# Adaptive layer norm, local attention and MLP on one core: half k-tiles of the first MLP product in 64-row tiles, singly given PSUM banks, norms on two engines

## The chip, the cores and the metric

One core of one Trainium2 chip runs the whole kernel. Five engines work side by side, each through its own list of instructions in order: TensorE (PE, matrix products into PSUM; the profile shows its weight loads as PEld), VectorE (DVE), ScalarE (ACT), GpSimd (POOL) and SyncE (SP, which issues most DMAs). The metric is the device time of one execution in microseconds, the median of several runs.

## The reference, cut to what matters

```python
mod = (silu(c) @ w_mod).reshape(1, 6, 1, 448)          # c is one row of 448
sa, ca, ga, sb, cb, gb = (mod[:, i] for i in range(6))
h = layernorm(x) * (1 + ca) + sa                       # x is 2048 x 448
q, k, v = split(h @ wqkv)                              # 16 heads of 28
logits[s, w] = q[s] . k[s - 2 w] * 28 ** -0.5          # w = 0..7; masked where s - 2 w < 0
x = x + ga * (softmax(logits) applied to v) @ wo
h = layernorm(x) * (1 + cb) + sb
x = x + gb * (gelu(layernorm(h) @ w1 + b1) @ w2 + b2)  # w1 is 448 x 1792, w2 1792 x 448
```

All inputs and the output are bfloat16.

## The kernel before, in words

**Tiles.** The 2048 tokens are put in an order in which even ones come before odd ones, so that the stride of 2 in the attention becomes 1. They are 16 blocks (`b`) of 128 tokens. The 448 features are `KT` = 4 k-tiles of 128 rows, the last of which holds 64. The weights and all activations between stages stay in SBUF.

**Stages.** In the opening c, the first x and the first weights are loaded; `ps_c` and `c_col` turn c into a column, `silu` follows, and `ps_sa`, `ps_ca` (`col_fn`, L453) make sa and ca as columns, which `mod1` (L459 to L462) copies out. `front_end` takes x in groups of 2, 2, 4, 4, 4 blocks: statistics (L396, L406), `rstd` (L413 on DVE, L416 on POOL), `normalize` (L421) into `zbuf`, a transpose by PE (L517) or by DMA, modulation into `hT` (L526 on ACT, L529 on DVE), and the eight products `qk` (L539) that are copied to qT and kT (`copy`, L384 on DVE, L386 on ACT). `mod_item` (L563) makes the four other modulation vectors; ga and gb are multiplied into wo and w2. `attention(g)`, 17 times over 121 queries: logits `lt` (L613), exp (L624), mask product (L633), `pv` (L648), `po` (L658), division (`on`, L669), transpose `pt` (L679), copy `ot`. `wo_item` (L700) and the residual (L705) follow for each block, and `norm_items` for each two: two layer norms, with a modulation between them, and a DMA transpose (L739) into `yT`.

**The MLP** (`mlp_items`) is done in four chunks of 512 tokens. `w1_c.q`, for seven q, makes two of the 14 output tiles of 128 rows: four k-tiles each, so eight matmuls of 512 columns (L755). In the last k-tile, rows 0 to 63 are features 384 to 447, row 64 (`KA`) is b1 with a constant one in `ybuf`, and the rest is zero. One GELU (L762) takes both tiles, 1024 columns. `w2_b.q` (L778) adds them up for each of four blocks, and `fin`, `out` finish a block.

**PSUM** is eight banks. Pool `ps_lt` has two tiles of two banks (logits, x transposes, w1 outputs), `ps_s` three of one bank (all else), `ps_p2` one (w2's sums).

**The order** is made at build time. Each step is an operation in `Plan`, with the engines that can do it and a cost for each, what it needs, and the buffers that it takes. `order` is a list scheduler: it picks the operation that can start first, less a small weight for what lies behind it, with the hand-given offsets `PRI` and `NUDGE`; an operation with two engines gets the one that would end first by these costs. `LANDS` are assumed times at which loads have landed. `PHASES` tells how many attention steps come ahead of each chunk's w1. The engines run the resulting lists in order, and on the chip an operation waits for what it needs.

Of the kernel before, what the change touches and what calls it, by code (L numbers as in the profile page):

```python
# [16 lines left out]
KT = 4  # L17
KA = 64
# [14 lines left out]
PHASES = [9, 14, 17, 17]  # L33
W2S = [(0, 5), (5, 10), (10, 14)]
SLOTS = {"lt": 2, "s": 3, "p2": 1, "et": 2, "on": 2, "vb": 3, "z2": 2, "yT": 2, "hm": 2}

LANDS = [("c", 3.0), ("x0", 5.0), ("x2", 5.8), ("wmsa", 6.4), ("wmca", 7.2), ("wk", 8.4), ("wq", 9.4), ("later", 10.0),
         ("wv", 10.4), ("x4", 12.5), ("wmod2", 18.0), ("wo", 19.5), ("b2", 20.5), ("x8", 22.0), ("w1", 28.0),
         ("w2", 33.0)]

NIDLE = [11, 4]
PLANS = None

LOOK = 0.000121

PRI = {"ad": -181.5, "agfst": -82.1, "ags2": -347.3, "ex": -137.9, "ge": -154.4, "h": -94.5, "lt": 209.3,
       "mk": -29.7, "ml": 177.8, "on": -459.2, "po": -127.9, "pv": -157.8, "r2": 73.3, "r3": -46.8, "s2": -114.2,
       "s3": -56.5, "ve": 41.4, "w1": -75.6, "w2": -12.0, "wo": 472.9, "wq": 377.0, "x1": 437.8, "y": -137.1,
       "yt": 24.4, "z": -134.6, "z2": 11.3, "zt": 143.7}

NUDGE = {"ad12": 15.6, "ad2": -30.3, "ad8": 44.8, "agfst12": -48.8, "agfst6": 98.9, "ags2_13": -79.7,
       "ags2_14": 66.3, "ags2_15": -24.2, "ags2_2": 13.3, "ags2_8": 84.1, "ags3_13": 100.2, "ags3_14": -12.2,
       "ex14.1": 144.5, "fin2": 21.9, "ge2.0": -4.6, "ge3.3": -73.9, "h2.2": 280.0, "lt10": 82.1, "lt8": -96.4,
       "mk16": -4.1, "mk3": 236.6, "ml0": 45.3, "ml12": 24.2, "ml6": -123.2, "on16": -89.1, "on4": -65.7,
       "on9": 60.2, "ot11": 20.9, "ot2": 66.5, "ot3": -126.0, "ot4": -23.7, "out1": 36.4, "out14": 29.2,
       "out15": -322.5, "out2": 24.7, "out9": -87.4, "po16": 38.4, "po9": 49.4, "pt16": 16.3, "pt2": 36.7,
       "pt3": -118.5, "pv13": -326.1, "pv16": 12.1, "qe0.0": 77.8, "qe0.6": -60.5, "qe12.5": 124.2,
       "qe2.5": 111.3, "qe8.0": 142.3, "qe8.3": 117.4, "qk2.5": 255.7, "qk8.0": 142.4, "qk8.1": 138.6,
       "r2_10": 7.9, "r2_12": 207.3, "r2_14": 18.8, "r2_14a": 2.8, "r2_4a": 155.1, "r2_8": -68.9, "r2_8a": 87.6,
       "r3_0a": -13.7, "r3_10a": -65.1, "r3_12": -63.0, "r3_12a": 43.9, "r3_14": 28.5, "r3_14a": -10.2,  # L60
       "r3_8": -10.6, "rd15": 41.6, "rd16": -89.1, "s2_1": 61.5, "s2_12": -57.7, "s2_13": -42.9, "s2_15": -4.9,
       "s2_3": 68.8, "s2_9": -35.4, "s3_12": 65.1, "s3_14": 46.0, "w1_0.6": 31.3, "w1_1.5": 58.9,
       "w1_3.3": -59.1, "w2_0.6": 121.6, "w2_1.4": 61.0, "w2_11.0": 60.4, "w2_11.3": -105.2, "w2_11.4": -4.4,
       "w2_11.5": 45.1, "w2_11.6": 30.7, "w2_12.5": -140.6, "w2_13.2": -158.9, "w2_14.1": -6.6, "w2_14.3": -1.2,
       "w2_14.4": 47.8, "w2_14.5": 147.1, "w2_2.5": 20.1, "w2_4.2": -47.2, "w2_5.2": -7.0, "w2_5.3": -24.7,
       "w2_5.5": 19.2, "w2_5.6": -17.6, "w2_6.1": 3.9, "w2_6.2": 12.3, "w2_6.6": 5.9, "w2_8.0": -68.8,
       "w2_8.3": -69.5, "w2_8.5": 91.6, "w2_9.3": 69.1, "wo1": 88.2, "wo12": -28.3, "wo2": 44.1, "x1_1": 34.4,
       "x1_13": -39.6, "x1_3": -114.7, "y1": 51.8, "y10": 10.9, "y12": 102.0, "y13": -21.9, "y14": 13.4,
       "y3": 128.0, "yt12": -52.1, "yt13": 30.6, "yt14": 12.1, "yt9": 260.3, "z2_1": 79.9, "z2_12": 15.9,
       "z2_13": 66.8, "z2_14": 106.9, "z2_15": 45.5, "z2_4": 123.4, "z2_6": -29.2}  # L70
# [9 lines left out]
class Plan:  # L80
# [8 lines left out]
    def add(self, name, eng, needs=(), after=(), uses=(), allocs=(), lag=0.09, tab=None, at=0.0, fn=None, pri=0.0):  # L89

        i = len(self.ops)
        self.index[name] = i
        self.ops.append(dict(name=name, eng=eng, needs=list(needs), after=list(after), allocs=list(allocs), lag=lag,
                             tab=tab, at=at, fn=fn, pri=pri + PRI.get(re.match(r"[a-z]+([0-9](?=_))?", name)[0], 0.0) +
                             NUDGE.get(name, 0.0)))
        for b in list(uses) + list(allocs):
            self.bufs[b][1].append(i)

    def order(self, hop=0.07, table=1.3, win=3.413):
# [27 lines left out]
        tab = None  # L127
# [6 lines left out]

        def slot_time(t, extra=0):
            k = len(turn[t]) + extra - self.slots[t]
            if k < 0:
                return 0.0
            b = turn[t][k] if k < len(turn[t]) else None
            if b is None or any(end[u] is None for u in users[b]):  # L140
                return None
            return max(end[u] for u in users[b]) + hop

        while ready:
            best = None
            for i in ready:
# [7 lines left out]
                ok, cntt = True, {}  # L154
                for b in o["allocs"]:
                    tg = tag_of[b]
                    st = slot_time(tg, cntt.get(tg, 0))
                    cntt[tg] = cntt.get(tg, 0) + 1
                    if st is None:
                        ok = False  # L160
                        break
                    t = max(t, st)
# [4 lines left out]
                s = max(t, free[e])  # L167
# [3 lines left out]
                if best is None or key < best[0]:  # L171
                    best = (key, i, e, s)
            assert best is not None, [ops[i]["name"] for i in ready]
            _, i, e, s = best
            o = ops[i]
            d = o["eng"][e]
            if e == "PE":
                w = int(s / win)
# [11 lines left out]
            for b in o["allocs"]:  # L190
                turn[tag_of[b]].append(b)
# [14 lines left out]
def kernel(  # L206
# [39 lines left out]

    cst = ctx.enter_context(tc.tile_pool(name="cst", bufs=1))
    ps_lt = ctx.enter_context(tc.tile_pool(name="ps_lt", bufs=2, space=bass.MemoryType.PSUM))
    ps_s = ctx.enter_context(tc.tile_pool(name="ps_s", bufs=SLOTS["s"], space=bass.MemoryType.PSUM))
    ps_p2 = ctx.enter_context(tc.tile_pool(name="ps_p2", bufs=SLOTS["p2"], space=bass.MemoryType.PSUM))  # L250

    def ps_att(shape, dtype, name):
        return ps_s.tile(shape, dtype, name=name, tag="s")

    ps_small = ps_att
# [35 lines left out]
    b2_bc = cst.tile([128, D], BF16, name="b2_bc")  # L291
    silu_bf = cst.tile([128, KT], BF16, name="silu_bf")
# [9 lines left out]
    wmod = stp.tile([128, KT, 2, D], BF16, name="wmod")  # L302
    wqk_st = stp.tile([128, KT, 2 * D], BF16, name="wqk_st")
    nc.scalar.dma_start(out=x_all[:, 0:2, :], in_=xv[:, 0, 0:2, :])
    load_ktiles(nc.sync, wmod[:, :, 0, :], w_mod[:, 0:D], 0)
    load_ktiles(nc.scalar, wmod[:, :, 1, :], w_mod[:, D:2 * D], 0)
    nc.scalar.dma_start(out=x_all[:, 2:4, :], in_=xv[:, 0, 2:4, :])
    load_ktiles(nc.sync, wqk_st[:, :, D:2 * D], A_wqkv[:, D:2 * D], 0)
    load_ktiles(nc.sync, wqk_st[:, :, 0:D], A_wqkv[:, 0:D], 0)
# [4 lines left out]
    nc.sync.dma_start(out=b2_bc[:], in_=B_b2.partition_broadcast(128))  # L314
    nc.sync.dma_start(out=x_all[:, 8:NBLK, :], in_=xv[:, 1, :, :])
# [6 lines left out]
    def idle(n):  # L322
        for i in range(n):
            idle_ps = ps_att([128, 512], FP32, "idle_ps")
            nc.tensor.matmul(idle_ps[:], lhsT=idle_in[:, 0:128], rhs=idle_in[:], start=True, stop=True)

    idle(4)
# [5 lines left out]
    nc.vector.memset(w1_s[64:128, KT - 1, :], 0.0)  # L333
    nc.gpsimd.memset(neg_half[:], -0.5)
    warm = stp.tile([128, 1], FP32, name="warm")
    nc.scalar.activation(out=warm[:], in_=neg_half[:, 0:1], func=ACT.Exp)
    nc.gpsimd.memset(ident[:], 0.0)
# [28 lines left out]
    nc.vector.memset(ca1_col[64:128, KT - 1:KT], 0.0)  # L366
    nc.vector.memset(sa_col[64:128, KT - 1:KT], 0.0)
    for vb in vbufs:
        nc.gpsimd.memset(vb[:, :, DH:DH + 1], 1.0)
    for yb in ybufs:  # L370
        nc.gpsimd.memset(yb[:, D:DP], 0.0)
        nc.gpsimd.memset(yb[:, D:D + 1], 1.0)
    load_ktiles(nc.sync, w1_s, B_w1, 0)
    nc.sync.dma_start(out=w1_s[KA:KA + 1, KT - 1, :], in_=B_b1.rearrange("(o n) -> o n", o=1))
# [35 lines left out]
    def rstd(nm, tile_key, n, **kw):  # L410
        def a_fn(e):
            tv = T["tv", tile_key] = sm.tile([128, n], FP32, name="tv", tag=f"tv{n}")
            nc.vector.tensor_scalar_add(out=tv[:], in0=T["mv", tile_key][:, :, 1], scalar1=EPS)  # L413
        def fn(e):
            rs = T["rs", tile_key] = sm.tile([128, n], FP32, name="rs", tag=f"rs{n}")
            nc.gpsimd.tensor_tensor(out=rs[:], in0=T["tv", tile_key][:], in1=neg_half[:, 0:n], op=ALU.pow)  # L416
        P.add(nm + "a", {"DVE": 0.08}, fn=a_fn, **kw)
        P.add(nm, {"POOL": 0.75}, lag=0.02, needs=[nm + "a"], fn=fn)

    def normalize(dst, src, tile_key, i):  # L420
# [10 lines left out]
    def c_fn(e):  # L431
        T["ps_c"] = ps_s.tile([128, KT], FP32, name="ps_c", tag="s")
# [14 lines left out]
    def col_fn(v):  # L447
        if v == 0:
            T["ps_col"] = ps_s.tile([128, 2 * KT], FP32, name="ps_col", tag="s")
        for j in range(KT):  # L450
            nj = kr_of(j)
            for kt in range(KT):
                nc.tensor.matmul(T["ps_col"][0:nj, v * KT + j:v * KT + j + 1],  # L453
                                 lhsT=wmod[0:kr_of(kt), kt, v, j * 128:j * 128 + nj],
# [405 lines left out]
```

## Time and profile before

| | us |
|---|---|
| median of 3 runs | 190.64 (190.16 to 190.86) |
| profiled execution | 190.52 |
| its span, first to last instruction | 188.8 |
| PE busy | 179.8 (1446 matmul records) |
| DVE busy | 140.3 |
| ACT busy | 105.4 |
| first `pq` (L539) starts | 13.28 |
| first w1 product (L755) starts | 71.39 |

A group such as `L755 PE MATMUL p<-yT,w_s 128*128 128x512 bf16 x8` is eight matmuls of line 755 that use 128 rows and 128 columns of the array and move 512 columns. The busy time of a matmul is longer than the distance to the next one's start, since matmuls overlap in the pipeline; the distances tell what a matmul costs. A few matmul records are missing, so a group may count one too few. In a row of the stages (`13.00:71.00 ...`) the columns are length, then busy us and instructions of PE, PEld, DVE, ACT and POOL, then the granted clock, DMA share and GB/s.

### The profile page before, as it was taken

Reading aid. Unit: us, or ns where it says so; the run is one execution under the profiler, and the core shown is the slowest. Engines: PE = TensorE matmul, PEld = TensorE weight load, DVE = VectorE, ACT = ScalarE, POOL = GpSimd, SP = SyncE. Lnnn points to the kernel's source line nnn. Section 1 sums busy time; section 2 is a strip of 40 time slices with the busy share of each in tenths; the row PEclk is TensorE's granted clock in tenths of the full one; section 3 lists DMA queues with packets and bytes.
Section 4 is the critical chain, followed back from the end, with each engine's and each line's share of the span. In section 5 each row is a group of like instructions: output and inputs, shape, how many; then the busy total and the mean of one; then the engine's idle time right before and its main releaser. Section 6 shows DMA issues by size and latency. Waiting matters only on the chain.

```text
span 188.8 us, 3664 instructions
## 1 busy us (share of the span) xinstructions
PE 179.8 (95%) x1446; PEld 94.5 (50%) x1460; DVE 140.3 (74%) x344; ACT 105.4 (56%) x149; POOL 23.7 (13%) x53
## 2 busy tenths in 40 slices
PE   7989899899999898999999999999999999999993
PEld 2658644445544444445556544456554444444551
DVE  5688799996998999967989998399999602202451
ACT  3048687587777866558744575868364444251100
POOL 7132002200104100311030103100103100000000
PEclk9969999999999999999999999999999999999999
DMA  5999992541001150004013002120000220000021
GB/s 178 302 375 295 406 309 89 111 83 33 0 3 28 28 61 0 0 0 59 24 43 65 0 28 53 32 50 3 26 30 28 54 56 24 3 24 0 28 70 49
DMA packets 23285, 14.40 MB, mean 76 GB/s; under 512 B 13666, under 2 KB 22371, under 8 KB 23268
## 3 DMA queue, kind: packets, MB, share of 16 engines
q1 hardware_dynamic: 22244, 13.31, 26.6%
q10 hardware_dynamic: 1024, 0.86, 1.4%
q8 instruction: 11, 0.18, 0.4%
q14 instruction: 6, 0.05, 0.1%
HBM read 9.18 MB, written 1.84 MB: 58 GB/s over the span
## 4 chain that ended last, share of the span: by engine, by line
PE 72%; DVE 15%; DMA 5%; POOL 2%; issue 2%; ACT 1%; ACTq 1%; DVEq 0%
PE p L755 25%; PE p L778 23%; PE pw L700 6%; DVE st L396 5%; PE pv L648 4%; PE pq L539 4%; DMA x_all<-in_A_x_dram 3%; PE lt L613 2%; PE pt L679 2%; POOL rs L416 2%; PE po L658 2%; DMA yT<-ybuf 2%; PE ptr L517 1%; DVE hT L529 1%; DVE zbuf L421 1%
## 5 line engine op out<-in xcount | busy, mean ns | idle before, releaser
L755 PE MATMUL p<-yT,w_s 128*128 128x512 bf16 x216 | 50.5, 379 | 1.1 <-DMA yT<-ybuf 0.7
L778 PE MATMUL p<-w_s,hm 128*128 128x448 bf16 x224 | 48.3, 352 | 0.1
L762 ACT ACTIVATE hm<-p 128x1024 bf16<-128x1024 f32 x28 | 28.6, 1024 | 31.6 <-PE p L755 29.5
L624 ACT ACTIVATE et<-lt 128x1024 bf16<-128x1024 f32 x34 | 33.9, 1029 | 9.1 <-PE lt L613 9.1
L416 POOL TENSOR_TENSOR rs<-tv,neg_half 128x2 f32<-128x2 f32 (+1 forms) x21 | 20.0, 954 | 125.1 <-DVE tv L413 102.5
L755 PEld LDWEIGHTS <-w_s 128*128 128x128 bf16 x224 | 21.6, 98 | 25.9 <-issue 1.1
L778 PEld LDWEIGHTS <-hm 128*128 128x128 bf16 x224 | 21.1, 98 | 19.0
L539 PE MATMUL pq<-hT,Wqk 128*128 128x512 bf16 (+1 forms) x155 | 29.2, 335 | 0.8 <-DVE qT L384 0.6
L791 DVE TENSOR_TENSOR xt<-p,gbb_bc 128x448 f32<-128x448 f32 x11 | 6.8, 622 | 27.0 <-PE p L778 26.9
L539 PEld LDWEIGHTS <-Wqk 128*128 128x128 bf16 x160 | 15.3, 98 | 12.0 <-issue 1.1
L633 DVE TENSOR_TENSOR et<-et,mask_rest 128x2048 bf16<-128x2048 bf16 x17 | 20.6, 1209 | 0.2 <-ACT et L624 0.2
L396 DVE BATCH_NORM_STATS2 st<-x_all 128x6 f32<-128x448 bf16 x30 | 17.8, 615 | 1.6 <-DMA x_all<-in_A_x_dram 1.4
L700 PE MATMUL pw<-wo_s,oT 128*128 128x448 bf16 x64 | 14.8, 353 | 0.5 <-ACT oT L386 0.3
L648 PE MATMUL pv<-Wv,hT 128*128 128x448 bf16 x68 | 15.0, 353 | 0.0
L386 ACT CAST kT<-pq 128x512 bf16<-128x512 f32 (+1 forms) x19 | 9.6, 508 | 4.6 <-PE pq L539 4.1
L705 DVE TENSOR_TENSOR x_all<-pw,x_all 128x448 bf16<-128x448 f32 x16 | 9.8, 615 | 2.5 <-PE pw L700 2.3
L669 DVE TENSOR_TENSOR on<-po,rden 128x448 bf16<-128x448 f32 x17 | 10.5, 619 | 0.1
L386 ACT CAST vbuf<-pv 128x448 bf16<-128x448 f32 x15 | 7.8, 538 | 4.7 <-PE pv L648 4.7
L658 PEld LDWEIGHTS <-et 128*128 128x128 bf16 x272 | 9.0, 96 | 2.6 <-DVE x_all L705 0.2
L386 ACT CAST qT<-pq 128x512 bf16<-128x512 f32 (+1 forms) x18 | 9.1, 526 | 1.7 <-PE pq L539 1.2
L658 PE MATMUL po<-vbuf,et 128*128 128x29 bf16 x272 | 9.3, 176 | 0.0
L396 DVE BATCH_NORM_STATS2 st<-z 128x6 f32<-128x448 bf16 x16 | 9.2, 615 | 0.1
(101 smaller groups left out, 165.5 us busy)
## 6 DMA issues: line engine op xcount, KB each, us to landing
out_dram<-x_all SPq DMA_DIRECT2D x16, 112.0 KB, 1.7
w_s<-in_B_w_dram SPq DMA_DIRECT2D x1, 1568.0 KB, 13.4
wmod<-in_w_mod_dram SPq DMA_DIRECT2D x1, 1344.0 KB
w_s<-in_B_w_dram SPq DMA_DIRECT2D x1, 1344.0 KB, 14.4
x_all<-in_A_x_dram SPq DMA_DIRECT2D x1, 896.0 KB, 10.8
wqk_st<-in_A_wqkv_dram SPq DMA_DIRECT2D x2, 336.0 KB
x_all<-in_A_x_dram ACTq DMA_DIRECT2D x2, 224.0 KB, 4.3
x_all<-in_A_x_dram SPq DMA_DIRECT2D x1, 448.0 KB, 5.2
```

The source lines that it names most:

```text
L386: nc.scalar.copy(out=out, in_=in_)
L396: nc.vector.bn_stats(out=st[:], in_=src())
L416: nc.gpsimd.tensor_tensor(out=rs[:], in0=T["tv", tile_key][:], in1=neg_half[:, 0:n], op=ALU.pow)
L539: nc.tensor.matmul(pq[:, 0:w], lhsT=Wqk[:, kt, m, :], rhs=hT[:, kt, c0:c0 + w], start=(kt == 0), stop=(kt == KT - 1))
L624: nc.scalar.activation(out=et_v[:, 2 * half:2 * half + 2], in_=T["lt", g][half][:].rearrange("p r (ft c) -> p r ft c", ft=4), func=ACT.Exp ...
L633: nc.vector.tensor_tensor(out=et[:], in0=et[:], in1=mask_rest[:], op=ALU.mult)
L648: nc.tensor.matmul(pv[:], lhsT=hT[:, kt, k0:k0 + BK], rhs=Wv[:, kt, :], start=(kt == 0), stop=(kt == KT - 1))
L658: nc.tensor.matmul(po[:, h, :], lhsT=T["et", g][:, h, :], rhs=vbufs[g % NVB][:, h, :], start=True, stop=True)
L700: nc.tensor.matmul(pw[:], lhsT=oT[:, kt, jb * 128:(jb + 1) * 128], rhs=wo_s[:, kt, :], start=(kt == 0), stop=(kt == KT - 1))
L755: nc.tensor.matmul(p1[:, f, 0:w], lhsT=w1_s[:, kt, ft * 128:(ft + 1) * 128], rhs=T["yT", c][:, kt, 0:w], start=(kt == 0), stop=(kt == KT - 1))
L762: nc.scalar.activation(out=T["hm", c][:, 2 * q:2 * q + 2, 0:w], in_=T["p1", c, q][:, :, 0:w], func=ACT.Gelu_apprx_tanh)
L778: nc.tensor.matmul(T["p2", b][:], lhsT=T["hm", c][:, ft, bi * 128:(bi + 1) * 128], rhs=w2_s[:, ft, :], start=(ft == 0 and b not in XPE), s ...
```

## The change

**w1.** `ybuf` is now 512 wide and holds features 0 to 255 and 192 to 447, and w1 is loaded in the same way (`load_twice`). So k-tiles 0 and 3 are features 0 to 127 and 320 to 447, and features 192 to 255 stand twice, at the end of k-tile 1 and at the start of k-tile 2. Of a pair of outputs the first takes k-tiles 0, 3, 1 whole (`mains`) and rows 64 to 127 of k-tile 2 (`ends`); the second takes 0, 3, 2 whole and rows 0 to 63 of k-tile 1. `ends` is an operation of its own (`wt`) for two pairs, or one at a chunk's end, and counts as 64 rows. b1 is now the bias of GELU; a transpose (`b1_fn`) makes it a column. GELU takes one output tile, 512 columns, and follows `wt`.

**PSUM.** One pool of four two-bank tiles; `order` chooses for each buffer a single bank (`1`, `p2`) or an aligned pair (`2`) of the eight, and `ps_of`, `ps_pair` give it. w2's sums may have two banks.

**Norms.** `normalize` can run on ACT, as an activation with scale `rs` and bias `nb`; for this `rstd` makes the negative mean `ng` on DVE and `nb` = `ng` x `rs` on POOL, for every norm.

**The opening.** wq's load is issued by ACT after its first table load, the second x load by SP behind wk. `wmod` and `wmod2` are padded with zeros to four whole k-tiles, so `col_fn` and `mod_item` use 128 rows throughout, and `mod1` is two copies. Idle matmuls stand in four places (8, 3, 3, 4). `use_ga` is one product.

**The plan.** `order` knows the rows of a PE operation and adds `turn_over` where they change; `PHASES`, `LANDS`, `LOOK`, `PRI` and `NUDGE` have new values, so the order of all engines is a new one.

```diff
-PHASES = [9, 14, 17, 17]
+PHASES = [9, 16, 17, 17]
...
+    def load_twice(eng, dst, src):
+        a = eng.dma_start(out=dst[:, 0:2, :], in_=src[0:256, :].rearrange("(kt p) n -> p kt n", p=128))
+        b = eng.dma_start(out=dst[:, 2:4, :], in_=src[192:448, :].rearrange("(kt p) n -> p kt n", p=128))
+        return [a, b]
+    def twice(ap):
+        return bass.AP(ap.tensor, ap.offset, [ap.ap[0], [192, 2], [1, 256]])
+    def mains(outs, lhs, rhs):
+        for w, o in enumerate(outs):
+            for i, kt in enumerate((0, 3, 1 + w)):
+                nc.tensor.matmul(o, lhsT=lhs(w, slice(0, 128), kt), rhs=rhs(slice(0, 128), kt), start=(i == 0),
+                                 stop=False)
+    def ends(outs, lhs, rhs):
+        for w, (o, r, kt) in enumerate(zip(outs, (slice(64, 128), slice(0, 64)), (2, 1))):
+            nc.tensor.matmul(o, lhsT=lhs(w, r, kt), rhs=rhs(r, kt), start=False, stop=True)
...
-    ps_lt = ctx.enter_context(tc.tile_pool(name="ps_lt", bufs=2, space=bass.MemoryType.PSUM))
-    ps_s = ctx.enter_context(tc.tile_pool(name="ps_s", bufs=SLOTS["s"], space=bass.MemoryType.PSUM))
-    ps_p2 = ctx.enter_context(tc.tile_pool(name="ps_p2", bufs=SLOTS["p2"], space=bass.MemoryType.PSUM))
+    pool = ctx.enter_context(tc.tile_pool(name="psum", bufs=1, space=bass.MemoryType.PSUM))
+    psum = [pool.tile([128, 2, 512], FP32, name=f"ps{i}") for i in range(4)]
+    def ps_of(nm, n=512, rows=128):
+        k = P.bank[nm]
+        return psum[k // 2][0:rows, k % 2, 0:n]
...
-    nc.scalar.dma_start(out=x_all[:, 2:4, :], in_=xv[:, 0, 2:4, :])
     load_ktiles(nc.sync, wqk_st[:, :, D:2 * D], A_wqkv[:, D:2 * D], 0)
-    load_ktiles(nc.sync, wqk_st[:, :, 0:D], A_wqkv[:, 0:D], 0)
+    nc.sync.dma_start(out=x_all[:, 2:4, :], in_=xv[:, 0, 2:4, :])
...
+    nc.vector.memset(wmod[64:128, KT - 1, :, :], 0.0)
+    nc.vector.memset(wmod[:, :, :, D:DP], 0.0)
...
-    nc.vector.memset(w1_s[64:128, KT - 1, :], 0.0)
+    nc.vector.memset(wmod2[64:128, KT - 1, :], 0.0)
...
     nc.scalar.activation(out=warm[:], in_=neg_half[:, 0:1], func=ACT.Exp)
+    load_ktiles(nc.scalar, wqk_st[:, :, 0:D], A_wqkv[:, 0:D], 0)
...
-    load_ktiles(nc.sync, w1_s, B_w1, 0)
-    nc.sync.dma_start(out=w1_s[KA:KA + 1, KT - 1, :], in_=B_b1.rearrange("(o n) -> o n", o=1))
+    load_twice(nc.sync, w1_s, B_w1)
...
+            ng = T["nm", tile_key] = sm.tile([128, n], FP32, name="ng", tag=f"ng{n}")
+            nc.vector.tensor_scalar_mul(out=ng[:], in0=T["mv", tile_key][:, :, 0], scalar1=-1.0)
...
+            nc.gpsimd.tensor_tensor(out=nb[:], in0=T["nm", tile_key][:], in1=rs[:], op=ALU.mult)
...
-    def normalize(dst, src, tile_key, i):
+    def normalize(e, dst, src, tile_key, i):
+        if e == "ACT":
+            nc.scalar.activation(out=dst, in_=src, func=ACT.Identity, bias=T["nb", tile_key][:, i:i + 1],
+                                 scale=T["rs", tile_key][:, i:i + 1])
+            return
...
-            P.add(f"z2_{b}", {"DVE": 0.32}, needs=[f"r2_{k}"], after=[f"z2_{k}"] if i else [], fn=z_fn, **kw)
+            P.add(f"z2_{b}", {"DVE": 0.32, "ACT": 0.47}, needs=[f"r2_{k}"], after=[f"z2_{k}"] if i else [], fn=z_fn, **kw)
...
+        nc.scalar.activation(out=T["hm", c][:, ft, 0:w], in_=ps_of(f"p1_{c}.{ft}", w),
+                             func=ACT.Gelu_apprx_tanh, bias=b1_col[:, ft:ft + 1])
...
-                    for kt in range(KT):
-                        nc.tensor.matmul(p1[:, f, 0:w], lhsT=w1_s[:, kt, ft * 128:(ft + 1) * 128],
-                                         rhs=T["yT", c][:, kt, 0:w], start=(kt == 0), stop=(kt == KT - 1))
+                mains([ps_of(nm, w) for nm in p1s], lhs_of(q), rhs)
...
+            if q % 2 or q == FT // 2 - 1:
+                qs = [q - 1, q] if q % 2 else [q]
+                def t_fn(e, qs=qs):
+                    for q in qs:
+                        ends([ps_of(f"p1_{c}.{ft}", w) for ft in (2 * q, 2 * q + 1)], lhs_of(q), rhs)
+                P.add(f"wt_{c}.{q}", {"PE": len(qs) * w / 2400 + 0.02}, needs=[f"w1_{c}.{q}" for q in qs], rows=64,
+                      lag=0.17, uses=[f"yT{c}"] + [f"p1_{c}.{ft}" for ft in range(2 * qs[0], 2 * q + 2)], fn=t_fn)
```

## The prediction

> **What bounds the kernel now.** I read the page's busy time and slices first. In the first fence the rows are busy time (us, share of the span, instructions) and busy tenths in 40 slices of 4.7 us.
>
> ```profile
> PE   179.8 (95%) x1446; PEld 94.5 (50%) x1460; DVE 140.3 (74%) x344; ACT 105.4 (56%) x149; POOL 23.7 (13%) x53
> ...
> PE   7989899899999898999999999999999999999993
> ...
> DVE  5688799996998999967989998399999602202451
> ACT  3048687587777866558744575868364444251100
> PEclk9969999999999999999999999999999999999999
> ```
>
> PE is full nearly everywhere, but its share does not tell whether it works or waits in the matmul pipeline, so I read the pace of its instructions in the timeline (start, busy time, xcount).
>
> ```profile
> 35.67 0.40 PE L613 MATMUL lt<-qT,kT 28*128 28x128 bf16 x16
> 36.00 1.03 PE L563 MATMUL pb_cb<-wmod,silu_bc 128*128 128x448 bf16 x4
> 36.97 0.40 PE L679 MATMUL pt<-ident,on 128*128 128x128 bf16 x4
> 37.20 1.02 PE L563 MATMUL pb_sb<-wmod,silu_bc 128*128 128x448 bf16 x4
> ...
> 152.17 1.89 PE L755 MATMUL p<-yT,w_s 128*128 128x512 bf16 x8
> 153.90 0.54 PE L778 MATMUL p<-w_s,hm 128*128 128x448 bf16 x2
> 154.28 1.89 PE L755 MATMUL p<-yT,w_s 128*128 128x512 bf16 x8
> ```
>
> From start to start: eight 512-column matmuls take 153.90 - 152.17 = 1.73, or **0.216 us** each; a 448-column one (154.28 - 153.90) / 2 = 0.19; a transpose (37.20 - 36.97) / 4 = 0.057. Four 448-column matmuls should take 0.76, but pb_cb takes 36.97 - 36.00 = 0.97: its fourth matmul has only 64 rows (form 64*128), so the array changes its tile shape and back. That is **0.2 us for there and back**. The logits (L613) have 28 rows in four row positions: 16 matmuls of 128 columns take 0.33. At 0.057 each in turn they would need 0.9, so the four positions run side by side (4 rounds of 0.057, and 0.1 for a change of shape).
>
> Next, where PE stands still. From the first `pq` (L539, 13.28) to the first `p` L755 (71.39) I multiply counts by paces: pq 96 x 0.216 + 64 x 0.109, 80 matmuls of 448 columns x 0.19, 44 transposes x 0.057, 128 `po` x 0.0255, nine logit groups x 0.41 (their two changes within), four modulation groups' changes x 0.2: 53.1 us of work in 58.1, so **5.0 us lost**. From 71.39 to the last L778 (185.5) the same sum gives 114.0 of 114.1: nothing is lost there, and each microsecond less of PE work counts. The waits of PE from 12 to 72 us (total, times, longest) name who was late:
>
> ```profile
> PE pt L679 <- DVE on L669: 1.2, 2, 0.9
> PE p L755 <- DMA yT<-ybuf: 0.7, 1, 0.7
> PE pq L539 <- DVE qT L384: 0.6, 1, 0.6
> ```
>
> DVE itself, or a DMA that follows DVE's `y`. The stages (PE, PEld, DVE, ACT, POOL busy) agree, DVE 52.7 of 58:
>
> ```profile
> 13.00:71.00 58.00, 54.96 (x557) 30.69 (x559) 52.66 (x129) 43.77 (x72) 7.18 (x7) 1.00 0.47 126
> ```
>
> Before 13.28 the opening is bound by DVE and loads (timeline):
>
> ```profile
> 8.31 1.15 DVE L396 BATCH_NORM_STATS2 st<-x_all 128x6 f32<-128x448 bf16 x2 [1.45 <-DMA x_all<-in_A_x_dram]
> ...
> 10.92 0.15 DVE L459 TENSOR_SCALAR ca_col<-ps_col 128x3 f32<-128x3 f32 x1
> ...
> 11.30 1.48 ACT L526 ACTIVATE hT<-ptr,sa_col,ca_col 128x256 bf16<-128x256 bf16 x3 [6.54 <-DVE sa_col L462]
> ...
> 13.28 4.97 PE L539 MATMUL pq<-hT,Wqk 128*128 128x256 bf16 x44
> ```
>
> The columns `ps_col` were done at 9.5, but DVE came to them at 10.92, behind the second x load's statistics, the normalisations and copies of `Wqk`; ACT had idled 6.5 us.
>
> **The change, part by part.**
>
> *w1 in pairs.* Of 224 matmuls 168 stay whole, and 56 become 64-row ones, in 28 pairs on opposite halves of the array and in different PSUM banks. If a pair runs side by side, as the four positions of L613 do, it takes one 0.216: 224 x 0.216 becomes 168 x 0.216 + 28 x 0.216, **-6.05**. No row has a 64-row pair. Its bounds are 0.216 (beside each other) and 0.432 (in turn); I take 0.216, since L613's rows are the nearest: row tiles with their own banks.
>
> The skill page "TensorE: Matmul & The Clock Gate", section "Measured speedup vs the span model", gives 3.07 times for four row tiles, not 4. As an estimate, 77% efficiency would make a pair 0.28 and lose 1.8 us of the 6.05, for 187.4 in all. L613 shows nothing of that loss, and I go by it.
>
> *Changes of shape.* The 64-row matmuls are issued in 16 blocks (two pairs, the last of a chunk one); in the changed kernel's order two blocks touch, so 15 trips x 0.2 = **+3.0**. The modulation vectors' fourth k-tile is now zero-padded to 128 rows: -4 x 0.2 = **-0.8**. The transpose of b1 stands right behind a logit group, with the same tile shape: +0.06.
>
> *Order.* Eight transposes of x move from before the first pq to behind it: +0.45 on PE there, given back by an earlier first pq. So PE's work from the first pq on falls by 6.05 - 3.0 + 0.8 - 0.06 - 0.45 = **-3.3**; counted through the new order with the same paces, -1.6 before the first w1 matmul and -1.7 after it.
>
> *Opening.* DVE's memsets before `c_col` grow by about 0.8 (two for `wmod`: 64x512 words as L328's 0.48, and a small one; `wmod2`'s replaces `w1_s`'s of equal size), and silu ends near 6.1 instead of 5.4. wq's issue moves to ACT's queue ahead of `e_c` (two issues of 0.5), where x2's 0.8 stood: no later than the new `c_col`. x2 goes to SP behind wk, and DVE's statistics of it behind `mod1` and two `hT`: no longer in their way. `ps_col` loses its changes of shape (32 matmuls took 2.26). DVE: statistics of x0 6.1 to 7.7 with the new `ng`, `rs` (0.71 on POOL) 8.4, z0 8.8, z1 on ACT at the same time after the added `nb`; two `Wqk` copies, `mod1` 9.7; `hT` on ACT and DVE by 10.9. PE has seven idle matmuls in front, ended at 11.4 at full clock (0.216 each), 12.9 at half the clock (PEclk has 6 in the third slice, and L325's early 128x512 ran 0.43 apart). First pq between 10.9 and 13.3; I take 11.9: **-1.4**.
>
> *Norms on ACT.* Before the first w1, ten normalisations leave DVE (10 x 0.39), nine `ng` come (9 x 0.165), and the new order puts a mask product (1.2) and two `on` (1.2) behind the fourth `y`: DVE some 5 us lighter. ACT gets eight `z` and two `y`. The trace has no such ACT form: below, L399's 0.58 for 448 columns; above, `hT` 128x512 0.78. At 0.65, plus two Wqk copies, less two `hT`, +6 on 43.8. On POOL, nb adds between 0.1 (smallest memset) and 0.92 (another rs) to the ACT norms' chain alone. The 5.0 us of stalls can go to 2 (those that name DVE go) or 6.5 (ACT is late instead); with so full an ACT I take 4.5: **-0.5**.
>
> *GELU.* 28 instructions of 1024 columns (1.02) become 56 of 512; `kT`'s 512-column cast takes 0.59, so ACT gains 4.4 us over 115 in which it is busy about half. It waits now for the 64-row block, so four banks are held together. While ACT drains four (2.4), PE has six whole matmuls of the next pair, then six more (2.6) and w2 work; p2's slots and the singly given banks leave room for six. What is queued behind a w1 that lacks a bank is all of PE. Bounds 0 and +2 in the second stage; I take **+0.3**. The tail is safe: 94 w2 matmuls (18 us) follow the last w1 block.
>
> *Loads.* w1 is loaded with 64 rows twice, +0.22 MB; it is issued at 12 to 17 us and used at 66 or later, so its cover is 30 us. At the 295 GB/s of the page's fourth slice it would cost 0.8 without cover.
>
> **Sum**: -1.4 - 3.3 - 0.5 + 0.3 = **-4.9**. The profiled execution took 190.52 (span 188.8 and 1.7 around it), 0.1 under the median of 190.64: 190.5 - 4.9 = **185.6**.
>
> **Rivals.**
> 1. *The pairs take turns.* Place: each 64-row block. A 64-row modulation matmul alone takes as long as a whole one, so turns would give up all 6.05: 185.6 + 6.05 = 191.65, slower by 0.5%. It decides from a pair pitch of 0.39 (4.9 / 28 + 0.216), where the rest of the gain is eaten. L613 speaks against it.
> 2. *ACT becomes the bound before w1.* With 50 us in 55 it is late with `qT`, `kT` and `z`. Then that stage ends as late as now but for the opening: 190.5 - 1.4 - 1.7 + 0.3 = 187.7, or 189.5 if the opening gains nothing too. For it: the ACT slices of 6 to 8. Against: the new order takes two `hT` from it, and between 13 and 71 its idle time of 14 us is more than the 6 it gets.
> 3. *DVE was the only cause of the stalls.* They fall to 2 and pq starts at 11.2: 190.5 - 2.1 - 3.3 - 3.0 = 182.1.
>
> **How the numbers follow.** Forecast 185.6 (its own range 184 to 187.3): 0.58. Rival 2: 0.17. Rival 3: 0.16. Rival 1: 0.09. The unknown bounds alone reach from 182 to 188.6; with rival 2's upper end I give 182.0 to 189.5, leaving out the turns and the ends. About 0.5% is what a measurement can tell from no change (189.7 to 191.6). Faster holds the forecast, rival 3 and 0.12 of rival 2: 0.86. The rest of rival 2 and 0.02 of rival 1 lie within: 0.07. Slower is the rest of rival 1: 0.07.
>
> **What would show it.** After: the starts of two 64-row matmuls of a block a few ns apart and 0.216 to the next pair (step one); 0.1 before and after each block (two); modulation groups at 0.76 (three); first pq near 11.9; first w1 near 67 to 68; no PE wait of size after it. Wrong if pairs are 0.4 apart, if PE waits on ACT before 70 us, or if w1 waits for GELU.

## The result, and the profile after

The changed kernel takes **228.30 us** (median of 4 runs, 227.91 to 230.22) against 190.62 (190.16 to 190.86) before: ratio 1.200, interval 1.193 to 1.207. The forecast was 185.6, in a range of 182.0 to 189.5. Its profiled execution took 228.34 with a span of 226.6. The busy rows and PE's slices (5.7 us each now) of the page:

```profile
PE 183.6 (81%) x1464; PEld 90.2 (40%) x1464; DVE 137.7 (61%) x346; ACT 122.6 (54%) x190; POOL 27.9 (12%) x66
...
PE   7587993896889887799867799688889799978774
```

PE has hardly more work than before, but its slices are seldom 9: it stands still everywhere, and no other engine is full either. For every kernel I take three starts from the trace: the first `pq`, the first w1 matmul and the last w2 matmul. Between them, PE's work is the sum of counts and paces that the prediction used (53.2 and 113.6 us before, 51.5 and 111.8 in the changed order); what is over is lost. Behind the first w1 a matmul of 448 columns is taken at 0.189 instead of 0.19, so a loss is good to some 0.3 us.

| | first pq | first w1 | last w2 | lost ahead of w1 | lost behind it |
|---|---|---|---|---|---|
| before | 13.28 | 71.39 | 185.28 | 4.9 | 0.3 |
| changed | 12.60 | 82.16 | 223.08 | 18.1 | 29.1 |

So PE loses 47 us in place of 5. PE's waits (total, times, longest) over the whole span, where those of before held nothing over 1.4, name readers of PSUM:

```profile
PE ps L875 <- DVE xt L888: 5.4, 8, 0.8
PE ps L764 <- DVE wo_s L650: 2.7, 1, 2.7
PE ps L311 <- ACT hm L834: 2.5, 2, 1.4
PE ps L316 <- ACT hm L834: 2.1, 2, 1.3
PE ps L618 <- ACT qT L456: 1.7, 4, 0.9
PE ps L764 <- ACT vbuf L456: 1.6, 2, 0.9
...
PE ps L311 <- DVE x_all L790: 1.3, 1, 1.3
```

These pairs make no sense as data. A transpose `pt` (L764) needs nothing of `use_ga` (L650, writing `wo_s`), and w2's products (L875) need nothing of another block's `xt` (L888). The chain that ended last shows the second one in the tail (start, us, engine):

```profile
203.20 2.82 PE ps L875 x14
206.04 0.63 DVE xt L888
206.72 2.82 PE ps L875 x14
209.57 0.64 DVE xt L888
210.24 2.82 PE ps L875 x14
```

Two blocks' sums lie in different banks, and yet a block's first product starts only after the block ahead of it has been read: 206.72 - 203.20 = 3.52 between blocks of 14 x 0.189 = 2.65, so 0.87 is lost each time. The only thing that these sums share is the two-bank tile in which both banks lie. My theory at this point: **the program's waits are laid by tile, not by bank**, and four two-bank tiles turn the eight singly given banks into four.

Two of the predicted signs are there all the same. A row of the timeline has two pairs of 64-row matmuls:

```profile
99.22 0.60 PE L316 MATMUL ps<-yT,w_s 64*128 64x512 bf16 x4
99.76 1.47 PE L311 MATMUL ps<-yT,w_s 128*128 128x512 bf16 x6
```

The four start at 99.224, 99.227, 99.449 and 99.453, and L311 at 99.761. Two of a pair start 3 to 4 ns apart and the next pair 0.225 later, so a pair costs one matmul; 0.09 is left for the change of shape.

### The profile page after: what moved, and what is told of

It reads as the page before. It is cut to its first block, busy times and chain, and to the rows that moved or that the text cites. A ratio compares the mean times of both kernels' runs of the same rounds, so it can differ in the third digit from the quotient of the medians.

```text
span 226.6 us, 3796 instructions
## 1 busy us (share of the span) xinstructions
PE 183.6 (81%) x1464; PEld 90.2 (40%) x1464; DVE 137.7 (61%) x346; ACT 122.6 (54%) x190; POOL 27.9 (12%) x66
## 3 DMA queue, kind: packets, MB, share of 16 engines
q10 hardware_dynamic: 1232, 1.03, 1.5%
## 4 chain that ended last, share of the span: by engine, by line
PE 57%; DVE 18%; ACT 16%; issue 4%; POOL 3%; ACTq 0%; DVEq 0%; POOLq 0%
PE ps L875 17%; PE ps L311 14%; PE ps L618 6%; PE ps L733 5%; ACT hm L834 5%; PE ps L785 4%; ACT et L709 3%; PE ps L316 3%; DVE x_all L790 3%; POOL rs L489 2%; DVE st L466 2%; DVE xt L888 2%; PE ps L398 2%; PE ps L743 2%; ACT qT L456 2%
## 5 line engine op out<-in xcount | busy, mean ns | idle before, releaser
L875 PE MATMUL ps<-w_s,hm 128*128 128x448 bf16 x224 | 48.2, 352 | 9.7 <-DVE xt L888 5.4
L311 PE MATMUL ps<-yT,w_s 128*128 128x512 bf16 x168 | 39.6, 379 | 6.0 <-ACT hm L834 2.5
L834 ACT ACTIVATE hm<-ps,b_col 128x512 bf16<-128x512 f32 x56 | 35.0, 689 | 16.2 <-PE ps L311 6.6
L709 ACT ACTIVATE et<-ps 128x1024 bf16<-128x1024 f32 x34 | 33.1, 1027 | 3.2 <-PE ps L698 3.2
L875 PEld LDWEIGHTS <-hm 128*128 128x128 bf16 x224 | 21.4, 97 | 32.6 <-issue 13.9
L618 PE MATMUL ps<-hT,Wqk 128*128 128x512 bf16 (+1 forms) x160 | 30.7, 336 | 3.1 <-ACT qT L456 1.7
L888 DVE TENSOR_TENSOR xt<-ps,gbb_bc 128x448 f32<-128x448 f32 x11 | 6.9, 623 | 37.7 <-PE ps L875 21.9
L311 PEld LDWEIGHTS <-w_s 128*128 128x128 bf16 x168 | 15.4, 97 | 27.3 <-issue 10.0
L733 PE MATMUL ps<-Wv,hT 128*128 128x448 bf16 x68 | 16.1, 372 | 1.6 <-DVE x_all L790 0.9
L785 PE MATMUL ps<-wo_s,oT 128*128 128x448 bf16 x64 | 14.2, 352 | 2.8 <-ACT qT L456 0.8
L790 DVE TENSOR_TENSOR x_all<-ps,x_all 128x448 bf16<-128x448 f32 x16 | 9.6, 613 | 7.2 <-PE ps L316 2.5
L754 DVE TENSOR_TENSOR on<-ps,rden 128x448 bf16<-128x448 f32 x17 | 10.5, 619 | 4.2 <-PE ps L733 1.5
L764 PE MATMUL ps<-ident,on 128*128 128x128 bf16 x68 | 6.8, 223 | 6.2 <-DVE wo_s L650 2.7
L456 ACT CAST qT<-ps 128x512 bf16<-128x512 f32 (+1 forms) x19 | 9.2, 510 | 4.6 <-PE ps L618 3.8
```

Source lines behind the costliest of these rows:

```text
L311: nc.tensor.matmul(o, lhsT=lhs(w, slice(0, 128), kt), rhs=rhs(slice(0, 128), kt), start=(i == 0), stop=False)
L456: nc.scalar.copy(out=out, in_=in_)
L618: nc.tensor.matmul(pq, lhsT=Wqk[:, kt, m, :], rhs=hT[:, kt, c0:c0 + w], start=(kt == 0), stop=(kt == KT - 1))
L709: nc.scalar.activation(out=et_v[:, 2 * half:2 * half + 2], in_=T["lt", g][half][:].rearrange("p r (ft c) -> p r ft c", ft=4), func=ACT.Exp ...
L733: nc.tensor.matmul(pv, lhsT=hT[:, kt, k0:k0 + BK], rhs=Wv[:, kt, :], start=(kt == 0), stop=(kt == KT - 1))
L785: nc.tensor.matmul(pw, lhsT=oT[:, kt, jb * 128:(jb + 1) * 128], rhs=wo_s[:, kt, :], start=(kt == 0), stop=(kt == KT - 1))
```

## The experiments

**1. Eight tiles of one bank.** The same order, the same banks and engines; only the declaration is by bank. As an instruction is given one tile, the exponentials of 1024 columns become two of 512.

```diff
-    psum = [pool.tile([128, 2, 512], FP32, name=f"ps{i}") for i in range(4)]
+    psum = [pool.tile([128, 512], FP32, name=f"ps{i}") for i in range(8)]
...
-        return psum[k // 2][0:rows, k % 2, 0:n]
+        return psum[k][0:rows, 0:n]
...
-                nc.scalar.activation(out=et_v[:, 2 * half:2 * half + 2],
-                                     in_=T["lt", g][half][:].rearrange("p r (ft c) -> p r ft c", ft=4),
+                for j in range(2):
+                    nc.scalar.activation(out=et_v[:, 2 * half + j],
+                                         in_=T["lt", g][half][j][:].rearrange("p (ft c) -> p ft c", ft=4),
```

> The changed kernel with PSUM declared as eight tiles of one bank instead of four tiles of two; order, banks and engines stay as they are. Only the exp of a logits pair, which read two banks at once, is cut in two instructions of 512 columns (34 more on ACT, at 0.69 - 1.03 / 2 = 0.17 each some 6 us of ACT time), and a transposed x is addressed bank by bank. Theory A (a matmul into one bank waits for the reader of the other bank of the same tile, because the waits are laid by tile): the 0.87 us between the w2 blocks in the tail vanish, and so do most PE waits for DVE and ACT; 184 to 192 us. Rival B (the four banks that GELU holds until the 64-row block, and the singly given banks, are too few): the banks are the same, so 225 to 230 us. Rival C (the new order with its hand-given offsets is badly placed for real durations): the order is the same, so 220 us or more. Rival D (ACT is too full): more ACT work, so 229 us or more.

Measured: **188.71** (188.43 to 190.51), before 190.47; ratio 0.993 (0.990 to 0.995). 39.6 us of the loss are gone, and theory A holds. Busy rows and PE's slices are those of a full PE again, and in the timeline of the tail the blocks' products follow each other without a pause (the second fence):

```profile
PE 177.9 (95%) x1464; PEld 89.5 (48%) x1464; DVE 136.1 (73%) x346; ACT 122.6 (66%) x224; POOL 27.8 (15%) x66
...
PE   7789899999999999999899999999999999999993
```

```profile
165.58 15.31 PE L876 MATMUL ps<-w_s,hm 128*128 128x448 bf16 x80
167.69 0.62 DVE L889 TENSOR_TENSOR xt<-ps,gbb_bc 128x448 f32<-128x448 f32 x1 [6.90 <-PE ps L876]
```

DVE reads one bank at 167.69 while PE writes another. The skill page "PSUM — Partial Sum Buffer", section "PSUM bank collisions raise a hardware error", asks for semaphores by bank and quadrant; this trace agrees that one bank may be read beside another's writes, and the waits of the changed kernel were coarser than that.

**2. The other way round: before, with its four single banks in two tiles.** Order and rotation stay. In this kernel and all that follow, the 24 transposing DMAs (z of eight blocks into `hT`, y into `yT`) are plain copies of the same size, so those tokens are worked on untransposed.

```diff
-    ps_s = ctx.enter_context(tc.tile_pool(name="ps_s", bufs=SLOTS["s"], space=bass.MemoryType.PSUM))
-    ps_p2 = ctx.enter_context(tc.tile_pool(name="ps_p2", bufs=SLOTS["p2"], space=bass.MemoryType.PSUM))
+    two = [ps_4.tile([128, 2, 512], FP32, name=f"two{i}") for i in range(2)]
...
+    ps_s = Turn([(0, 0), (0, 1), (1, 0)])
+    ps_p2 = Turn([(1, 1)])
```

> The kernel before, its order and its rotation of banks kept, but the four banks that it gives out singly (three for the small products, one for w2's sums) are declared as two tiles of two banks; its transposing DMAs are plain copies. Nothing else is changed. Theory A (a product into one bank of a tile waits for the readers of the other bank): over 195, and PE waits for copies, additions and xt that read another bank. Rival (banks are told apart inside a tile, and the loss of the changed kernel came from its order or from something that the eight tiles changed beside it, such as the exponentials in two halves): 189.0 to 191.5, as before.

Measured: **215.68** (215.33 to 217.21), before 190.38; ratio 1.134 (1.130 to 1.137). Half of before's banks, paired in this way, cost 25.3 us, with none of the change's other parts. PE's waits show the same false pairs, here `pt` (L669) behind `use_ga` (L594) again:

```profile
PE two L669 <- DVE wo_s L594: 2.1, 1, 2.1
PE two L560 <- ACT qT L406: 1.6, 5, 0.5
```

Together the two runs settle the cause of the loss. What is left is why the kernel with eight tiles stands at 188.7 and not at 185.6.

**3. The base for what follows**: eight tiles, with the plain copies.

```diff
-                nc.sync.dma_start_transpose(out=T["yT", c][:, :, o:o + 128], in_=ybufs[b % NYB][:])
+                nc.sync.dma_start(out=T["yT", c][:, :, o:o + 128],
+                                  in_=ybufs[b % NYB][:].rearrange("p (kt n) -> p kt n", kt=KT))
```

> The kernel with eight one-bank tiles (188.71 us), but its 24 transposing DMAs (z of the last eight blocks into hT, y into yT) are plain copies of the same size from SBUF to SBUF, so q, k, v and the MLP of these tokens work on data that is not transposed. Everything else, the order too, is the same. It is the base for the next kernels. Theory A (the DMAs were early enough, only one wait of 0.4 us for them is in the trace): 188.0 to 189.0. Rival B (a plain copy takes longer than a transposing one and makes PE wait): over 189.5.

Measured: **187.99** (187.51 to 189.66), before 190.31; ratio 0.989 (0.984 to 0.993). The time is at the lower edge of A, so the copies don't slow the kernel.

**4. Whole w1.** Without pairs, without 64-row blocks; `ybuf` is 448 wide with zeros behind.

```diff
-            for i, kt in enumerate((0, 3, 1 + w)):
-                nc.tensor.matmul(o, lhsT=lhs(w, slice(0, 128), kt), rhs=rhs(slice(0, 128), kt), start=(i == 0),
-                                 stop=False)
+            for kt in range(KT):
+                nc.tensor.matmul(o, lhsT=lhs(w, slice(0, 128), kt), rhs=rhs(slice(0, 128), kt), start=(kt == 0),
+                                 stop=(kt == KT - 1))
```

> The base with plain copies, order and banks kept, but w1 whole again: 224 matmuls of 128 rows, zero rows in the last k-tile, no 64-row blocks. b1 stays the bias of GELU. The transposes by DMA are plain copies as in the base. Theory of the prediction (a pair costs one matmul, -6.05, and each of 15 trips to the 64-row shape 0.2, +3.0): 3.0 slower than the base (2.3 to 3.7). Rival (the trips and the later GELU eat the gain): -0.7 to +0.8. Rival (pairs in turn, so that only the trips are left): 2.2 to 3.2 faster than the base.

Measured: **191.54** (191.17 to 192.49), ratio 1.006 (1.004 to 1.009): 3.55 slower than the base. From the first pq to the last w2 it is 173.61 against 170.30, so 3.3. The prediction's net of -6.05 + 3.0 holds.

**5. More trips to the 64-row shape** (made on the kernel of experiment 7, 186.91). Each pair's two 64-row matmuls follow that pair at once.

```diff
                 mains([ps_of(nm, w) for nm in p1s], lhs_of(q), rhs)
+                if q % 2 == 0 and q < FT // 2 - 1:
+                    ends([ps_of(nm, w) for nm in p1s], lhs_of(q), rhs)
...
-                    for q in qs:
+                    for q in qs[-1:]:
```

> The kernel with wq on SP (plain copies, 186.91 us), but the two 64-row matmuls of every pair are issued right behind that pair's whole k-tiles, not for two pairs together: 27 trips to the 64-row shape in place of 15, the same matmuls. Theory of the prediction (0.2 for there and back, and PE is what sets the end): 12 x 0.19 = 2.3 slower (1.7 to 2.8). Rival (the earlier GELU of the first pair gives it back, or a trip hides in other waits): slower by under 1.2.

Measured: **189.22** (189.21 to 191.08), ratio 0.994 (0.992 to 0.996): 2.31 slower for 12 trips more, 0.19 each. The 0.2 is right by itself, and not only in the net.

**6. An earlier exponential of c, no idle matmuls ahead of pq.** In the base, `e_c` stands on ACT behind the issue of wq's load: it began at 6.10, though `c_col` was done at 5.4. wq comes in two parts. The large one (336 KB) was issued at 2.42, the small one (56 KB) only at 5.58, and `e_c` followed it.

```diff
-    load_ktiles(nc.scalar, wqk_st[:, :, 0:D], A_wqkv[:, 0:D], 0)
...
+    def ec_fn(e):
+        nc.scalar.activation(out=e_c[:], in_=c_col[:], func=ACT.Exp, scale=-1.0)
+        load_ktiles(nc.scalar, wqk_st[:, :, 0:D], A_wqkv[:, 0:D], 0)
...
-              fn=lambda e, nm=nm, n=n: idle(NIDLE[n], ps_of(nm)), pri=50.0)
+              fn=lambda e, nm=nm, n=n: idle(NIDLE[n] if n < 2 else 0, ps_of(nm)), pri=50.0)
```

> The base with plain copies, without the seven idle matmuls between the x transposes and the first pq, and with wq's load issued by ScalarE right behind the exponential of c instead of ahead of it. Theory A (PE was held by the idle matmuls at half clock up to 13.47, and the exponential waited at ScalarE behind that issue, from 5.4 to 6.24): exponential at 5.4, first pq at 11.6 to 11.8, 1.7 faster than the base (1.2 to 2.2). Rival B (the loads or the clock set the pace of the opening): first pq no earlier than 12.3, or at half clock until 15; within 0.9 of the base. Rival C (wq lands later and the first q products wait): slower than the base.

Measured: **192.77** (191.47 to 193.00), ratio 1.010 (1.006 to 1.014), 4.8 slower than the base. `e_c` ran at 5.42, as A had it, and the first pq at 10.57, earlier than A had it, and then C struck. ACT took up wq only at 15.69 (timeline; in the base at 11.56), and PE waited 3.3 us:

```profile
15.69 0.56 ACT L455 COPY Wqk<-wqk_st 128x448 bf16<-128x448 bf16 x1 [4.71 <-DMA wqk_st<-in_A_wqkv_dram]
```

wq's large part was now issued at 6.33 instead of 2.42, 3.9 us later, and took 9.3 us to land, where wk's, of the same size on SP, took 5.0. From 6 to 14 us the DMA engines had no pause (share 1.04 to 1.12); that SP's earlier loads held wq up is likely, but not shown by itself. The first products also ran slowly: the granted clock was 0.57 from 10 to 12 us. The run changed both the load and the idle matmuls, and doesn't tell their shares apart.

**7. wq on SP behind wk, idle matmuls in PE's pauses.** `e_c` waits for no issue on ACT; six idle matmuls instead of eight stand ahead of `ps_sa`, and seven more behind `ps_ca`.

```diff
     load_ktiles(nc.sync, wqk_st[:, :, D:2 * D], A_wqkv[:, D:2 * D], 0)
+    load_ktiles(nc.sync, wqk_st[:, :, 0:D], A_wqkv[:, 0:D], 0)
...
-    load_ktiles(nc.scalar, wqk_st[:, :, 0:D], A_wqkv[:, 0:D], 0)
...
+        if v == 1:
+            idle(7, psum[7][:])
```

> The base with plain copies, with wq's load back on SP right behind wk's (so the exponential of c waits for no issue at ScalarE), eight idle matmuls ahead of ps_sa cut to six and seven more behind ps_ca. Theory A (the opening is bound by the chain c, silu, statistics, z, transposes, hT, which starts 0.7 earlier): exponential at 5.4, first pq at 11.3 to 11.5 at full clock, 187.2 (186.7 to 187.7). Rival B (wq, x2 or Wv land later by the order of the loads, and the products or the second x group wait, as where the load was put behind the exponential): over 188.0.

Measured: **186.91** (186.90 to 187.18), before 190.38; ratio 0.981 (0.979 to 0.983): 1.1 faster than the base, as A had it. The timeline has the first pq at 11.38:

```profile
5.41 0.20 ACT L546 ACTIVATE e_c<-c_col 128x4 f32<-128x4 f32 x1 [1.58 <-DVE c_col L519]
...
9.87 1.67 PE L399 MATMUL ps<-idle_in 128*128 128x512 bf16 x7
...
11.38 3.66 PE L621 MATMUL ps<-hT,Wqk 128*128 128x256 bf16 x32
```

**8. Only the idle matmuls**: the base with five more behind `ps_ca`.

> The base with plain copies (187.99 us), and five more idle matmuls behind ps_ca, where PE stands still for 1.3 us before the x transposes. Theory A (that pause lets the clock fall in some executions, and the seven idle matmuls behind the transposes then run at half clock to 13.47 instead of 12.06): first pq at 12.0 to 12.2, clock full from 10 on, 187.6 (187.2 to 188.0), and runs closer together. Rival B (the pause doesn't decide the clock): within 0.3 of the base, first pq anywhere from 12.0 to 13.5.

Measured: **187.90** (187.82 to 189.07), ratio 0.987 (0.985 to 0.990): no different from the base, and a time that both A and B allowed. The clock was full from 8 us on, but the first pq came at 12.57, later than A had it, since in this execution ACT came to `e_c` at 6.60, behind the issue of wq. So the pause of PE does not tell the whole; the opening's chain counts as well, and experiment 7 moved both.

**9. Half of the exponentials' columns** from the tenth attention step on; the other weights are left from earlier steps. With it `et` becomes two fixed tiles.

```diff
-                    nc.scalar.activation(out=et_v[:, 2 * half + j],
+                    nf = 4 if g < 9 else 2
+                    nc.scalar.activation(out=et_v[:, 2 * half + j, 0:nf],
```

> The base with plain copies (187.99 us), but from the tenth attention step on the exponentials take only half of their columns (two of four feature tiles; the rest of the weights is left from earlier steps), which takes some 7 us of work from ScalarE behind the first w1. Order and waits stay. Theory A (the 3.3 us that PE loses behind the first w1 come from ScalarE being late, at the logits' banks above all): 1.5 to 3.0 faster. Rival B (they come from the order: VectorE's division, the y transposes, or a bank whose other reader is late): within 0.7.

Measured: **187.92** (187.09 to 189.30), ratio 0.987 (0.984 to 0.991), the base's time. From the first w1 to the last w2 it is 114.54 against 115.14, 0.6 less, which is what rival B allowed. Of the base's waits on ACT behind the first w1, the logits' for `et` (0.6) is gone, and those for GELU (0.4 and 0.2) stay. So shorter exponentials alone give little; it doesn't follow that ACT's lateness costs little, as the base's rows below show.

**10 and 11. All norms on DVE**, the order kept: first on the base, then on experiment 7's kernel.

```diff
     def normalize(e, dst, src, tile_key, i):
+        e = "DVE"
```

> The base with plain copies, its order kept, but every normalisation (z, z2, y) is done by VectorE at the same place of the order; the extra small products for ScalarE's form stay. Theory A (ScalarE's share of the norms is worth what the prediction gave it, some 0.5 us, since VectorE is the late one): 0.3 to 1.3 slower than the base. Rival B (ScalarE's norms are slow, 0.76 to 0.81 against VectorE's 0.40, and make somebody late): 0.3 to 0.9 faster. Rival C (they were all covered): within 0.3.

> The kernel with wq on SP (plain copies, 186.91 us), its order kept, with every normalisation done by VectorE at the same place of the order. Theory A (ScalarE's norms were covered and gave nothing, as with the earlier opening, where this was 0.1 slower with wide runs): within 0.3. Rival (they are worth the 0.5 us of the prediction): 0.4 to 1.0 slower.

Measured: **188.10** (187.13 to 188.36), 0.1 over the base; and **186.41** (186.28 to 186.80), ratio 0.979 (0.977 to 0.982), 0.5 under experiment 7. The first lies in C; the second in neither of its two expectations. Its interval touches that of experiment 7, though its slowest run (186.80) is under the fastest there (186.90). ScalarE's norms gave nothing and may have cost some tenths. Row groups of the kernel with eight tiles (busy, mean ns, idle before) show why they are no bargain; DVE's one of the same 512 columns took 0.41:

```profile
L497 ACT ACTIVATE ybuf<-z,nb,rs 128x512 bf16<-128x512 bf16 x9 | 7.2, 814 | 8.3 <-DMA yT<-ybuf 4.9 <-POOL nb L491 3.4
...
L497 ACT ACTIVATE z<-x_all,nb,rs 128x448 bf16<-128x448 bf16 x4 | 3.0, 760 | 4.8 <-POOL nb L491 4.8
```

Experiment 11 is the fastest that was run. With transposing DMAs it was not tried, so its time is that of a kernel that leaves the transposes out.

## Why the prediction was wrong, step by step

The same three starts for the kernels that the steps are read from, with full or half clock ahead of pq as noted:

| | first pq | first w1 | last w2 | lost ahead of w1 | lost behind it |
|---|---|---|---|---|---|
| eight tiles (clock 0.50 from 10 to 12 us) | 13.47 | 67.66 | 183.37 | 2.7 | 3.9 |
| base, plain copies (1.00) | 12.06 | 67.21 | 182.36 | 3.7 | 3.3 |
| wq on SP (1.00) | 11.38 | 66.52 | 181.66 | 3.6 | 3.3 |

- **GELU and banks, +0.3 (0 to +2): the step that failed.** It said that "p2's slots and the singly given banks leave room for six", took "what is queued behind a w1 that lacks a bank is all of PE" as the danger, and called the tail safe. The banks are given singly by the planner, but the waits hold a whole two-bank tile, so a product into one bank waits for the other bank's reader. This is no wait of w1 alone: it is at `pt`, `pq`, `pv`, `lt` and w2 too. It cost 39.6 us (experiment 1), 0.87 of it at each block of the tail that I had called safe. The mechanism was not among the rivals: each of them took the order of the banks as what the planner made of it. The planner's own costs had the same belief in them, so its order could not go around the waits.
- **The same step with its banks free.** Even with eight tiles PE loses 3.3 to 3.9 behind the first w1, where I had 0.3 on top of nothing: outside the bounds. The profile's waits on ACT add up to only 1.2 (`et` 0.6, GELU 0.6 in the base), because PE counts as idle only from the end of a matmul, and its busy time (0.379 for 512 columns) is longer than the distance to the next start (0.216). Read from start to start, the same waits cost more. Here are the base's two late groups of logits:

```profile
88.63 0.23 PE L699 MATMUL ps<-qT,kT 28*128 28x128 bf16 x2
89.19 0.21 PE L699 MATMUL ps<-qT,kT 28*128 28x128 bf16 x1 [0.34 <-ACT et L711]
89.68 0.38 PE L699 MATMUL ps<-qT,kT 28*128 28x128 bf16 x13 [0.28 <-ACT et L711]
90.00 1.31 PE L878 MATMUL ps<-w_s,hm 128*128 128x448 bf16 x6
...
125.04 0.43 PE L699 MATMUL ps<-qT,kT 28*128 28x128 bf16 x3
125.84 0.38 PE L699 MATMUL ps<-qT,kT 28*128 28x128 bf16 x13 [0.37 <-ACT hm L837]
126.15 1.12 PE L878 MATMUL ps<-w_s,hm 128*128 128x448 bf16 x5
```

They take 1.37 and 1.11 in place of 0.34, and four transposes ahead of a product that waits for GELU (78.44 to 79.02) take 0.58 in place of 0.23: 2.15 us lost to ACT's `et` and `hm`. Another 0.27 goes to DVE's `oT` at 79.6; some 0.9 in small gaps stays open. In experiment 9 the first group still takes 0.94 and the second 1.11. With the norms on DVE (experiments 10 and 11) both are back at 0.34, but DVE's `oT` and `et` now cost 1.15 and 0.47, and the stage is only 0.24 shorter (114.90): the norms make whichever engine has them late. GELU itself was 0.69 instead of 0.59, and the exponentials in two halves took 0.63 each, 1.26 for 1.03 before.
- **w1 in pairs, -6.05; changes of shape, +3.0: right.** Net 3.3 to 3.55 (experiment 4) against 3.05, and 0.19 per trip (experiment 5). The modulation groups are at 0.75 (37.72 to 38.47 with eight tiles) in place of 0.97, as the -0.8 had it. Rival 1 (pairs in turn) falls with the 3 to 4 ns between the starts of a pair. The discount that I had worked out from the page on TensorE (0.28 per pair) is not seen: 0.225.
- **Norms on ACT, -0.5: the gain is there, its cause is not.** Ahead of the first w1 PE loses 2.7 to 3.7 with eight tiles instead of 5.0, a larger gain than I gave; but with every norm on DVE the time is the same or lower (experiments 10 and 11). So it is not ScalarE that cut the stalls, but what else the change moved, its order and its banks; no run tells these two apart. I had the ACT form at 0.65; it takes 0.76 to 0.83. Rival 2 (ACT the bound before w1) gave 187.7 to 189.5, and eight tiles lie in that span, but not by its way: the loss ahead of w1 fell. Rival 3 (the loss there falls to 2) was near for this stage; its earlier pq (11.2) and the quiet stage behind w1 did not come.
- **Opening, -1.4: right as a possibility, wrong as a fixed number.** With the clock full, the first pq came at 12.06 in the base and 12.60 in the changed kernel; at half clock at 13.47, and at 14.28 in experiment 9, whose opening is the same. My two ends (11.4 and 12.9 for the end of the idle matmuls) were those two states, and I took a value near the good one. Also, silu ended at 6.9 to 7.1 (base, eight tiles) instead of 6.1, as `e_c` waited on ACT for the issue of wq's second part (5.58 in the base), which I had put "no later than the new `c_col`" (5.4). Experiment 7 removes both and gives the 11.38 and the narrow runs.
- **Loads, and order (+0.45): nothing seen against them.** The x transposes moved, and w1's load was there long before 67 us.
- **The sum.** With eight tiles the first w1 came at 67.66, inside the predicted 67 to 68. Against 185.6, 188.71 is 3.1 more: 1.6 of it in the opening (13.47 for 11.9), and the rest is what PE loses behind the first w1 less what it gained ahead of it. That the first w1 met the prediction is luck: the pq came 1.6 late, and the stage lost 2.7 where I had 4.5.
- **The range.** Two of its sums don't come out. Rival 2 without a gain in the opening is 190.5 - 1.7 + 0.3 = 189.1, not 189.5. And the bounds given for the opening (10.9 to 13.3), the stalls (2 to 6.5) and GELU (0 to +2) reach from 181.8 to 190.7 when they are added up, not from 182 to 188.6. Neither comes near 228.3.

On the clock, the rows come first: behind the same instructions, with idle times of PE as long in one as in the other (0.94 and 1.13 us in the base, 0.97 and 1.13 in experiment 9), it was 1.00 from 10 to 12 us in the base's profiled execution and 0.50 in that of experiment 9. The skill page "TensorE: Matmul & The Clock Gate", section "What's actually happening", tells that activity is judged in a window that runs freely and isn't tied to the kernel's start; that fits one program having both, and no run here measures the window.

## What to carry to other kernels

When buffers are made finer in the plan, make them finer in the declarations as well: what waits for what is decided by the object that the tracking knows, and a bank that shares a tile with another is not a bank of its own. In a profile, look for releasers that can't be data of the waiting instruction (a transpose released by a weight's scaling): they are the sign of it. To price a wait, read from start to start: PE's idle time leaves out what its pipeline covers, and here 1.2 us of waits cost 2.15. And moving a load's issue behind another instruction can cost far more than the half microsecond that an issue takes: wq's went from 2.42 to 6.33, and was in use 4.1 us later.

## What the runs showed that I had not expected

- Sharing a two-bank tile costs tens of microseconds even where the partner bank's reader is short: 39.6 us in one order and 25.3 in another, from waits that are mostly below 1.4 us each.
- Two 64-row matmuls in opposite halves of the array start 3 to 4 ns apart and cost 0.225 together, at 512 columns.
- Filling PE's pauses in the opening with idle matmuls changed nothing alone (187.90 against 187.99); with the chain shortened as well, the five runs lay within 0.3 us (186.90 to 187.18), where the base's six lay within 2.2.
- The norms cost much the same on either engine: on ScalarE they make PE wait for `et` and `hm`, on VectorE for `oT` and `et`.
